# Block-causal attention followed by a channel mix: from two stages with x in DRAM to one interleaved program with x on chip

## The chip, the core and the metric

The kernel runs on one core of a Trainium2 chip. The core has five engines that run at the same time and wait for each other by semaphores: TensorE (PE, matrix multiplication; loads of its stationary operand are shown as PEld), VectorE (DVE), ScalarE (ACT), GpSimd (POOL) and SyncE (SP), which here only issues DMAs. Work passes through SBUF (128 partitions) and PSUM (8 banks of 128 x 2 KB), where matmul results land. The metric is device time of one execution in microseconds.

## The reference

There are 8 batches of 8 heads, 576 positions and 64 channels a head, all float32. Attention is causal by blocks of 64 positions. Its output, with the heads side by side as 512 channels, is x of a channel mix that shifts by one position:

```
S  = q k^T / 8, kept where i // 64 >= j // 64      # i the query, j the key
x  = (exp(S) / row sum) v                          # (8, 576, 512)
xk = mu_k x + (1 - mu_k) x_prev                    # x_prev: x one position earlier, 0 at the start of a batch
xr = mu_r x + (1 - mu_r) x_prev
out = sigmoid(xr w_r) * (relu(xk w_k)^2 w_v)       # w_k 512x1024, w_v 1024x512, w_r 512x512
```

Matmul operands are 16-bit, sums are float32.

## The kernel before

The program has two stages, one after the other.

**Stage 1, attention (lines 74 to 180), a loop over 8 batches.** q and k are loaded by GpSimd's queue with a cast to bfloat16 (lines 88 and 92), 128 positions to a partition tile, so that a row of 64 numbers is the unit that lies together. PE transposes them in blocks of 128 columns (line 103), VectorE copies the halves to KT and QT (lines 108, 110), both on partitions 0 to 63. v is loaded and cast the same way (lines 115, 119) beside columns of ones (line 122). Then a loop over 8 heads: six score matmuls (line 134) of keys against queries, 1600 columns in all, into one PSUM buffer; exp on ScalarE in two pieces (lines 147, 149); GpSimd zeroes what the mask removes (line 152); then PE multiplies with v as the stationary operand and exp as the moving one (lines 157, 162, 166), into one PSUM buffer PA. Row 64 of PA holds the row sums. ScalarE copies the 64 channel rows to XTB (line 169), VectorE the row sums to LTB (line 171). At a batch's end x, not yet normalised and transposed (channels on partitions), goes to DRAM with the row sums (lines 172, 173). After the last batch all row sums come back, VectorE takes reciprocals (line 179) and these go to DRAM.

**Stage 2, channel mix (lines 185 to 275), a loop over 4 pairs of batches.** SP loads x and, repeated over partitions, the reciprocals (lines 203, 207). VectorE multiplies them (line 216), GpSimd subtracts neighbours (DT, line 224), VectorE makes XK and XR (lines 226, 229). PE multiplies XK with WK (PK, line 238), ScalarE takes the relu (line 244), VectorE the square (line 246). Then for chunks of 128 positions: PR (line 261), sigmoid (line 265), PV (line 269), the product (line 273) and the store (line 275).

**What sets the order.** The program is written as loops over tiles from pools. The tile layer inserts the semaphores, and a planner orders each engine's instructions: program order is the priority, and an instruction whose inputs or buffers are late by the planner's own reckoning can be placed behind later ones. On the chip each engine, and each DMA queue, then runs its list in that fixed order. The order around the change is therefore the planner's, not one written by hand. A pool's `bufs` says how many tiles of a tag can be alive at once.

Of the kernel before, what the change touches and what calls it, by code (L numbers as in the profile page):

```python
# [9 lines left out]
FP = mybir.dt.float32  # L10
F16 = mybir.dt.float16
# [6 lines left out]
def kernel(  # L18
# [12 lines left out]
    nc = tc.nc  # L31
# [4 lines left out]
    SC = (H * S) // P  # L36
    CCn = C // P
    JCn = DF // P
    assert S == 576 and D == 64 and C == 512

    consts = ctx.enter_context(tc.tile_pool(name="consts", bufs=1))
    drams = ctx.enter_context(tc.tile_pool(name="drams", bufs=1, space=bass.MemoryType.DRAM))

    ident = consts.tile([P, P], BF)
    make_identity(nc, ident)

    xT_dram = drams.tile([P, CCn, B * S], FP)

    with tc.tile_pool(name="wstg", bufs=1) as wstg:
        WKs = wstg.tile([P, CCn, DF], FP)  # L50
        nc.sync.dma_start(WKs, moe_w_k.rearrange("(cc p) j -> p cc j", p=P))
        WK = consts.tile([P, CCn, DF], F16)
        nc.vector.tensor_copy(WK, WKs)
        WVs = wstg.tile([P, JCn, C], FP)
        nc.sync.dma_start(WVs, moe_w_v.rearrange("(cc p) j -> p cc j", p=P))
        WV = consts.tile([P, JCn, C], F16)
        nc.vector.tensor_copy(WV, WVs)
        WRs = wstg.tile([P, CCn, C], FP)
        nc.sync.dma_start(WRs, moe_w_r.rearrange("(cc p) j -> p cc j", p=P))
        WR = consts.tile([P, CCn, C], F16)  # L60
        nc.vector.tensor_copy(WR, WRs)
    MUK = consts.tile([P, CCn], FP)
    nc.sync.dma_start(MUK, moe_mu_k.rearrange("(cc p) -> p cc", p=P))
    MUR = consts.tile([P, CCn], FP)
    nc.sync.dma_start(MUR, moe_mu_r.rearrange("(cc p) -> p cc", p=P))
    l_dram = drams.tile([B * H, S], FP)
    ri_dram = drams.tile([B * H, S], FP)

    QS = [0, 128, 256, 384, 512]
    CS = [0, 576, 1024, 1344, 1536]  # L70
    NE = 1600
    ISQ = float(1.0 / (D ** 0.5))

    with (
        tc.tile_pool(name="qk", bufs=2) as qk_pool,
        tc.tile_pool(name="tr", bufs=2) as tr_pool,
        tc.tile_pool(name="vp", bufs=2) as v_pool,
        tc.tile_pool(name="ep", bufs=2) as e_pool,
        tc.tile_pool(name="xo", bufs=3) as xo_pool,
        tc.tile_pool(name="xtb", bufs=2) as xtb_pool,  # L80
        tc.tile_pool(name="pstr", bufs=2, space=bass.MemoryType.PSUM) as ps_tr,
        tc.tile_pool(name="pss", bufs=1, space=bass.MemoryType.PSUM) as ps_s,
        tc.tile_pool(name="psav", bufs=1, space=bass.MemoryType.PSUM) as ps_av,
    ):
        RB = 6
# [220 lines left out]
```

## Time and profile before

| | us |
|---|---|
| three runs | 501.98, 505.07, 505.12 |
| median | 505.07 |
| span of the profiled execution, first to last instruction | 498.2 |
| busy PE / VectorE / ScalarE / GpSimd in it | 368.1 / 268.6 / 212.6 / 156.1 |

Of the profiled execution the span is given and not its own device time. The three runs lie 3.8 to 6.9 us above that span.

How to read the profile: the page gives, for one execution, each engine's busy time, the span in 40 slices with the granted TensorE clock (PEclk, as a share of 2.4 GHz), the DMA queues and the groups of instructions that cost most. A group is named by line, engine, operation, and output <- inputs, with partitions x elements, its count, busy time and the mean duration of one. Matmuls are pipelined, and a matmul's duration has the drain of its result in it: 8 matmuls in a row take less than 8 durations. PE's busy time is the union of these durations, so a busy PE can still stream at half its rate. "Idle before" is the time in which an engine waited ahead of a group, with what ended the wait.

### The profile page before, as it was taken

The numbers are of one execution on the slowest core, as the hardware profiler recorded it, in microseconds if no ns is written. First come the engines' busy times: TensorE is split into PE (matmuls) and PEld (weight loads), VectorE is DVE, ScalarE is ACT, GpSimd is POOL, SyncE is SP. The second block draws the span as 40 slices with busy tenths as digits, with TensorE's granted clock in tenths as the row PEclk, the third lists the DMA queues.
The fourth block names the chain that finished last, engine by engine and source line by source line (L and its number), as shares of the span: only waits on it lengthen the run. The fifth ranks groups of instructions, "written<-read, shape, count | busy, mean of one in ns | idle before, by whom it ended". The sixth has DMA issues, their size and how long they took to land.

```text
span 498.2 us, 5776 instructions
## 1 busy us (share of the span) xinstructions
PE 368.1 (74%) x2112; PEld 194.4 (39%) x2112; DVE 268.6 (54%) x360; ACT 212.6 (43%) x330; POOL 156.1 (31%) x342
## 2 busy tenths in 40 slices
PE   0008798897979798889960005987968988999996
PEld 0005455463635455544430001543434434544642
DVE  2207544362726355632223159989799889625622
ACT  1002665665666658776640000731344125415621
POOL 9432417264454625341110035043343321000000
PEclk9999856675685759765555556998999999999999
DMA  9999999999499999191107989036882220121022
GB/s 284 215 133 108 126 32 147 94 140 100 104 122 86 131 36 145 23 123 39 59 18 278 269 215 289 0 91 179 234 225 45 95 78 7 42 107 42 22 93 75
DMA packets 132891, 57.95 MB, mean 116 GB/s; under 512 B 113784, under 2 KB 113784, under 8 KB 132856
## 3 DMA queue, kind: packets, MB, share of 16 engines
q0 software_dynamic: 111488, 14.16, 61.6%
q1 hardware_dynamic: 21376, 43.44, 29.1%
q8 instruction: 16, 0.26, 0.2%
q14 instruction: 11, 0.09, 0.1%
HBM read 52.58 MB, written 19.17 MB: 144 GB/s over the span
## 4 chain that ended last, share of the span: by engine, by line
PE 47%; DVE 19%; DMA 12%; ACT 9%; issue 7%; POOL 6%; SPq 0%; ACTq 0%; DVEq 0%; POOLq 0%
PE PV L269 11%; PE PA L157 9%; PE PS L134 9%; PE PK L238 6%; PE PR L261 5%; DVE K L246 4%; ACT E L147 4%; DVE XR L229 4%; DMA VO<-in_v_dram 4%; DVE LTB L171 4%; DVE XK L226 3%; PE pst L103 3%; ACT XTB L169 3%; DMA QKN<-in_k_dram 3%; DMA RB<-ri_dram 3%
## 5 line engine op out<-in xcount | busy, mean ns | idle before, releaser
L171 DVE COPY LTB<-PA 1x576 f32<-1x576 f32 x64 | 48.1, 751 | 109.3 <-ACT XTB L169 109.3
L238 PE MATMUL PK<-XK,WK 128*128 128x384 f16 (+2 forms) x384 | 67.5, 333 | 47.5 <-DVE XK L226 40.2
L147 ACT ACTIVATE E<-PS 128x1024 f16<-128x1024 f32 x64 | 65.5, 1023 | 82.4 <-PE PS L134 79.3
L134 PE MATMUL PS<-QT,KT 64*128 64x64 bf16 (+4 forms) x384 | 81.2, 362 | 9.5 <-ACT E L149 8.5
L269 PE MATMUL PV<-WV,K 128*128 128x512 f16 x320 | 76.7, 383 | 9.0 <-DVE OV L273 9.0
L157 PE MATMUL PA<-E,VO 128*128 128x512 f16 (+3 forms) x256 | 71.1, 421 | 14.7 <-DVE LTB L171 12.2
L244 ACT ACTIVATE KRj<-PK 128x512 f32<-128x512 f32 (+2 forms) x96 | 46.4, 491 | 81.1 <-PE PK L238 63.3
L224 POOL TENSOR_TENSOR DT<-XT 128x1154 f32<-128x1154 f32 x16 | 44.3, 2784 | 112.5 <-DVE XT L216 82.6
L238 PEld LDWEIGHTS <-WK 128*128 128x128 f16 x384 | 37.6, 98 | 77.3 <-issue 53.1
L152 POOL MEMSET E<- 64x64 f16 x256 | 29.3, 152 | 114.6 <-ACT E L147 99.8
L103 PE MATMUL pst<-ident,QKN 128*128 128x128 bf16 x288 | 31.1, 270 | 41.6 <-DMA QKN<-in_k_dram 38.6
L265 ACT ACTIVATE Rt<-PR 128x512 f32<-128x512 f32 (+1 forms) x40 | 23.7, 596 | 80.9 <-PE PR L261 55.3
L169 ACT COPY XTB<-PA 64x576 f32<-64x576 f32 x64 | 40.4, 631 | 35.3 <-PE PA L166 34.1
L134 PEld LDWEIGHTS <-KT 64*128 64x128 bf16 x384 | 38.1, 117 | 44.4 <-issue 30.6
L246 DVE TENSOR_TENSOR K<-KRj 128x512 f16<-128x512 f32 (+2 forms) x96 | 49.4, 567 | 3.1 <-ACT KRj L244 2.3
L269 PEld LDWEIGHTS <-K 128*128 128x128 f16 x320 | 31.5, 98 | 48.4 <-issue 12.1
L273 DVE TENSOR_TENSOR OV<-Rt,PV 128x512 f32<-128x512 f32 (+1 forms) x40 | 27.2, 683 | 38.4 <-PE PV L269 37.8
L157 PEld LDWEIGHTS <-VO 128*128 128x128 f16 x256 | 27.3, 125 | 49.8 <-issue 24.1
L261 PE MATMUL PR<-WR,XR 128*128 128x512 f16 x160 | 43.1, 390 | 3.8 <-DVE XR L229 3.8
L108 DVE COPY KT<-pst 64x768 bf16<-64x768 bf16 x48 | 26.4, 549 | 28.9 <-PE pst L103 28.0
L149 ACT ACTIVATE E<-PS 128x576 f16<-128x576 f32 x64 | 41.3, 645 | 0.0
L103 PEld LDWEIGHTS <-QKN 128*128 128x128 bf16 x288 | 22.7, 121 | 47.3 <-issue 44.0
(29 smaller groups left out, 289.7 us busy)
## 6 DMA issues: line engine op xcount, KB each, us to landing
xT_dram<-XTB SPq DMA_DIRECT2D x8, 1152.0 KB, 6.8
XTu<-xT_dram SPq DMA_DIRECT2D x8, 1152.0 KB, 8.0
RB<-ri_dram SPq DMA_DIRECT2D x16, 576.0 KB, 6.7
out_dram<-OV SPq DMA_DIRECT2D x32, 256.0 KB, 2.0
QKN<-in_q_dram POOLq DMA_DIRECT2D x8, 576.0 KB, 8.1
QKN<-in_k_dram POOLq DMA_DIRECT2D x8, 576.0 KB, 9.8
VO<-in_v_dram POOLq DMA_DIRECT2D x32, 128.0 KB, 8.9
WKs<-in_moe_w_k_dram SPq DMA_DIRECT2D x1, 2048.0 KB
```

Source lines behind the costliest of these rows:

```text
L103: nc.tensor.matmul(pst[:, i, :], QKN[:, blk + i, :, :].rearrange("p a b -> p (a b)"), ident, is_transpose=True, start=(i == 0), stop=(i == ...
L134: nc.tensor.matmul(PS[:, col:col + (q1 - q0)], KT[0:D, s0 + kc * P: s0 + (kc + 1) * P], QT[0:D, s0 + q0: s0 + q1], start=start, stop=stop)
L147: nc.scalar.activation(E[:, 0:1024], PS[:, 0:1024], AF.Exp, scale=ISQ)
L157: nc.tensor.matmul(PA[:, QS[kc]:512], Vc[:, kc], E[:, CS[kc]:CS[kc] + 512 - QS[kc]], start=(kc == 0), stop=(kc == 3))
L169: nc.scalar.copy(XTB[(h % 2) * D:(h % 2) * D + D, h // 2, :], PA[0:D, :])
L171: nc.vector.tensor_copy(LTB[0:1, h, :], PA[D:D + 1, :])
L224: nc.gpsimd.tensor_tensor(DT[:, 1:TT], XT[:, cc, 1:TT], XT[:, cc, 0:TT - 1], ALU.subtract)
L238: nc.tensor.matmul(PK[:, 0:t1 - t0], WK[:, cc, jc * P:(jc + 1) * P], XK[:, cc, t0:t1], start=(cc == 0), stop=(cc == CCn - 1))
L244: nc.scalar.activation(KRj[:, 0:t1 - t0], PK[:, 0:t1 - t0], AF.Relu)
L246: nc.vector.tensor_tensor(K2[:, jc, t0:t1], KRj[:, 0:t1 - t0], KRj[:, 0:t1 - t0], ALU.mult)
L261: nc.tensor.matmul(PR, XR[:, cc, ws:ws + P], WR[:, cc, :], start=(cc == 0), stop=(cc == CCn - 1))
L269: nc.tensor.matmul(PV, K2[:, jc, ws:ws + P], WV[:, jc, :], start=(jc == 0), stop=(jc == JCn - 1))
```

## The change

The two stages become one program of slots, 13 to a batch.

- q and k are loaded through SP's queue in float32, six positions of a head to a partition, so that 1536 bytes lie together; v as well, in rows of 256 bytes. GpSimd casts them to 16 bit. Two heads share the 128 partitions of QT and KT: even heads on 0 to 63, odd heads on 64 to 127.
- Scores of a pair of heads are made in three pieces of 2 x 512 columns; the last block of 64 keys of all heads of a batch is one more piece. exp takes 1024 columns at a time.
- For the product with v, exp tiles of 128 keys x 128 queries are the stationary operand and v with a column of ones (65 columns) the moving one. So queries are on partitions, the row sum is a column, and VectorE normalises out of PSUM. The last key block's exp lies in a tile that is zero elsewhere.
- x stays in SBUF. PE transposes it (float32) into chunks of 512 positions that run on across batches; each chunk keeps the column ahead of it.
- The weights are cast by the DMA; sigmoid(z) becomes (tanh(z / 2) + 1) / 2, with the half folded into WV.
- A batch's attention pieces are written alternately with the channel-mix matmuls ("units") of the chunk before, at slots given by hand; the planner still orders each engine from that. All PSUM but the scores' comes from one pool of four one-bank buffers (tag m).

The core of the diff (removed lines are those printed above):

```diff
+    ld_pool = pool("ld", 4)
+    vl_pool = pool("vl", 3)
...
+    kr_pool = pool("kr", 3)
+    k2_pool = pool("k2", 1)
+    o_pool = pool("op", 3)
+    ps_s = pool("pss", 2, space=PSUM)
+    ps_m = pool("psm", 4, space=PSUM)
...
+    VOs = [consts.tile([P, 5, H, D1 + 1], F16, name=f"VO{i}") for i in range(2)]
+    E4s = [consts.tile([P, H, P], F16, name=f"EL{i}") for i in range(2)]
+    QN, KN, QT, KT = {}, {}, {}, {}
...
+    def load_qk(b):
+        for hh in range(2):
+            for n, src in enumerate((q, k)):
+                LD[b, n, hh] = ld_pool.tile([PQ, HP, R, D], FP, tag="ld",
+                                            name="LD")
+                for h in range(0, HP, 2):
+                    nc.sync.dma_start(
+                        LD[b, n, hh][:, h:h + 2],
+                        src[b, hh * HP + h:hh * HP + h + 2].rearrange(
+                            "h (p r) d -> p h r d", r=R))
+    def cast_qk(b, hh, h):
+        for n, (dst, tag) in enumerate(((QN, "qn"), (KN, "kn"))):
+            if h == 0:
+                dst[b, hh] = qk_pool.tile([PQ, R, HP, D], BF, tag=tag, bufs=2,
+                                          name="QKN")
+            nc.gpsimd.tensor_copy(
+                dst[b, hh][:, :, h:h + 2].rearrange("p r h d -> p h r d"),
+                LD[b, n, hh][:, h:h + 2])
...
+    def load_v(b):
+        for sc in range(5):
+            n = P if sc < 4 else D
+            VL[b, sc] = vl_pool.tile([P, H, D], FP, tag="vl", name="VL")
+            nc.sync.dma_start(
+                VL[b, sc][0:n],
+                v[b, :, sc * P:sc * P + n].rearrange("h p d -> p h d"))
+    def cast_v(b, sc):
+        n = P if sc < 4 else D
+        nc.gpsimd.tensor_copy(VOs[b % 2][0:n, sc, :, 0:D], VL[b, sc][0:n])
...
+    def load_w():
+        nc.gpsimd.dma_start(WK, moe_w_k.rearrange("(cc p) j -> p cc j", p=P))
+        nc.gpsimd.dma_start(WR, moe_w_r.rearrange("(cc p) j -> p cc j", p=P))
+        nc.gpsimd.dma_start(WV, moe_w_v.rearrange("(cc p) j -> p cc j", p=P))
+        nc.vector.tensor_scalar_mul(WV, WV, 0.5)
+        nc.vector.tensor_scalar_add(MUK, MUK, -1.0)
+        nc.vector.tensor_scalar_add(MUR, MUR, -1.0)
+    def qk_transpose(b, pr):
+        if pr == 0:
+            QT[b] = tr_pool.tile([P, HP, S], BF, tag="qt", name="QT")
+            KT[b] = tr_pool.tile([P, HP * S + D], BF, tag="kt", name="KT")
+            nc.vector.memset(KT[b][:, HP * S:], 0.0)
+        for which in range(2):
+            N = (QN, KN)[which][b, pr // 2]
+            pst = ps_m.tile([P, CH], FP, tag="m", name="PQK")[:, :].bitcast(BF)
+            view = pst[:, 0:S].rearrange("p (r t) -> p t r", r=R)
+            for r in range(R):
+                nc.tensor.matmul(
+                    pst[:, r * PQ:(r + 1) * PQ], N[:, r, pr % 2 * 2:pr % 2 * 2 + 2, :].rearrange(
+                        "p h d -> p (h d)"),
+                    identb[0:PQ, 0:PQ], is_transpose=True,
+                    start=(r == 0), stop=(r == R - 1))
+            if which == 0:
+                nc.scalar.copy(
+                    QT[b][:, pr].rearrange("p (t r) -> p t r", r=R), view)
+            else:
+                    KT[b][:, pr * S:(pr + 1) * S].rearrange(
+                        "p (t r) -> p t r", r=R), view)
+    PIECES = [
+        [(0, 0, 0, 512)],
+        [(0, 0, 512, 64), (64, 1, 128, 448)],
+        [(0, 2, 256, 320), (320, 3, 384, 192)],
+    ]
+    ZEROS = [[0], [64], [0, 320]]
+    EP = {}
+    def score(b, pr, i):
+        if i == 0:
+            EP[b, pr] = e_pool.tile([P, 2, 3, 512], F16, tag="e", name="E")
+        E = EP[b, pr]
+        PS = ps_s.tile([P, 2, 512], FP, tag="s", name="PS")
+        for (col, kc, q0, n) in PIECES[i]:
+            for h in range(2):
+                rows = slice(h * D, h * D + D)
+                nc.tensor.matmul(
+                    PS[:, h, col:col + n],
+                    KT[b][rows, pr * S + kc * P: pr * S + (kc + 1) * P],
+                    QT[b][rows, pr, q0:q0 + n], start=True, stop=True)
+        nc.scalar.activation(E[:, :, i, :], PS, AF.Exp, scale=ISQ)
+        for z in ZEROS[i]:
+            nc.gpsimd.memset(E[D:P, :, i, z:z + D], 0.0)
+    def score_last(b):
+        E4 = E4s[b % 2]
+        PS = ps_s.tile([P, 2, 512], FP, tag="s", name="PS4")
+        for pr in range(HP):
+            for h in range(2):
+                rows = slice(h * D, h * D + D)
+                nc.tensor.matmul(
+                    PS[:, h, pr * D:pr * D + D],
+                    KT[b][rows, pr * S + 512: pr * S + 640],
+                    QT[b][rows, pr, 512:576], start=True, stop=True)
+        nc.scalar.activation(
+            E4[0:D, :, D:P].rearrange("p (a h) q -> p h a q", h=2),
+            PS[0:D, :, 0:HP * D].rearrange("p h (a q) -> p h a q", q=D),
+            AF.Exp, scale=ISQ)
+    def stationary(b, h, kc, m):
+        E = EP[b, h // 2][:, h % 2].rearrange("p i n -> p (i n)")
+        if kc == 4:
+            return E4s[b % 2][:, h, :]
+        base = (0, 576, 1024, 1344)[kc]
+        c = base + (448 if m == 4 else m * P) - kc * P
+        return E[:, c:c + P]
+    def av_norm(b, h):
+        if h == 0:
+            x_all[b] = x_pool.tile([P, 5, C], FP, tag="x", name="X")
+        VO = VOs[b % 2]
+        PA = ps_m.tile([P, CH], FP, tag="m", name="PA")
+        for m in range(5):
+            for kc in range(m + 1):
+                nc.tensor.matmul(
+                    PA[:, m * D1:(m + 1) * D1], stationary(b, h, kc, m),
+                    VO[:, kc, h, 0:D1], start=(kc == 0), stop=(kc == m))
+        Rc = r_pool.tile([P, 5], FP, tag="r", name="Rc")
+        view = PA[:, 0:5 * D1].rearrange("p (m e) -> p m e", e=D1)
+        nc.vector.reciprocal(Rc, view[:, :, D])
+        nc.vector.tensor_tensor(
+            x_all[b][:, :, h * D:(h + 1) * D], view[:, :, 0:D],
+            Rc[:, :].unsqueeze(2).to_broadcast([P, 5, D]), ALU.mult)
+    def x_transpose(b, m):
+        g0 = b * S + m * P
+        rows = P if m < 4 else D
+        off = 0 if m < 4 else D
+        px = ps_m.tile([P, CH], FP, tag="m", name="PX")
+        for cc in range(CCn):
+            nc.tensor.matmul(
+                px[:, cc * P:(cc + 1) * P],
+                x_all[b][:, m, cc * P:(cc + 1) * P], identf,
+                is_transpose=True, start=(cc == 0), stop=(cc == CCn - 1))
...
+            nc.scalar.copy(XT[c][:, :, 1 + t:1 + t + n],
+                           view[:, :, off + done:off + done + n])
+            done += n
+    def mix(c):
+        x = XT[c]
+        XK = xk_pool.tile([P, CCn, CH], F16, tag="xk", name="XK")
+        XR = xk_pool.tile([P, CCn, CH], F16, tag="xr", name="XR")
+        for cc in range(CCn):
+            DT = d_pool.tile([P, CH], FP, tag="d", name="DT")
+            nc.gpsimd.tensor_tensor(DT, x[:, cc, 1:CH + 1], x[:, cc, 0:CH],
+                                    ALU.subtract)
+            for b in range(B):
+                t = b * S - c * CH
+                if 0 <= t < CH:
+                    nc.gpsimd.tensor_copy(DT[:, t:t + 1],
+                                          x[:, cc, t + 1:t + 2])
+            for (dst, mu) in ((XK, MUK), (XR, MUR)):
+                    dst[:, cc], DT, mu[:, cc:cc + 1],
+                    x[:, cc, 1:CH + 1], ALU.mult, ALU.add)
+        XKR[c] = (XK, XR)
+    def pk(c, jc):
+        if jc == 0:
+            K2[c] = k2_pool.tile([P, JCn, CH], F16, tag="k2", name="K2")
+        ps = ps_m.tile([P, CH], FP, tag="m", name="PK")
+        for cc in range(CCn):
+            nc.tensor.matmul(ps, WK[:, cc, jc * P:(jc + 1) * P],
+                             XKR[c][0][:, cc], start=(cc == 0),
+                             stop=(cc == CCn - 1))
+        KR = kr_pool.tile([P, CH], FP, tag="kr", name="KR")
+        nc.scalar.activation(KR, ps, AF.Relu)
+        nc.vector.tensor_tensor(K2[c][:, jc], KR, KR, ALU.mult)
+    def prr(c, jt):
+        ps = ps_m.tile([P, CH], FP, tag="m", name="PR")
+        for cc in range(CCn):
+            nc.tensor.matmul(ps, XKR[c][1][:, cc, jt * P:(jt + 1) * P],
+                             WR[:, cc], start=(cc == 0), stop=(cc == CCn - 1))
+        T[c, jt] = t_pool.tile([P, CH], FP, tag="t", name="T")
+        nc.scalar.activation(T[c, jt], ps, AF.Tanh, scale=0.5)
+    def pv(c, jt):
+        ps = ps_m.tile([P, CH], FP, tag="m", name="PV")
+        for jc in range(JCn):
+            nc.tensor.matmul(ps, K2[c][:, jc, jt * P:(jt + 1) * P],
+                             WV[:, jc], start=(jc == 0), stop=(jc == JCn - 1))
+        OV = o_pool.tile([P, CH], FP, tag="o", name="OV")
+        nc.vector.scalar_tensor_tensor(OV, T[c, jt], 1.0, ps, ALU.add,
+                                       ALU.mult)
+        g = c * CH + jt * P
+        nc.sync.dma_start(o2[g:g + P], OV)
+    NP_ = 13
+    slots = {}
+    def at(slot, fn, *args):
+        slots.setdefault(slot, []).append((fn, args))
+    for b in range(B):
+        s0 = b * NP_
+        order = [("s", 0, 0), ("s", 0, 1), ("s", 0, 2), ("l",)] + [
+            ("s", pr, i) for pr in range(1, HP) for i in range(3)]
+        for n, o in enumerate(order):
+            if o[0] == "l":
+                at(s0 + n, score_last, b)
+            else:
+                at(s0 + n, score, b, o[1], o[2])
+            if b + 1 < B:
+                if n == 0:
+                    at(s0, load_qk, b + 1)
+                if n in (3, 5, 7, 9):
+                    at(s0 + n, cast_qk, b + 1, (n - 3) // 4, (n - 3) % 4)
+                if n == 3 and b == 0:
+                    at(s0 + n, load_w)
+                if n == 4:
+                    at(s0 + n, load_v, b + 1)
+                if n in (8, 9, 10, 11, 12):
+                    at(s0 + n, cast_v, b + 1, n - 8)
+                if n in (6, 8, 10, 12):
+                    at(s0 + n, qk_transpose, b + 1, (n - 6) // 2)
+        for pr in range(HP):
+            done = 3 if pr == 0 else 3 + 3 * pr
+            at(s0 + done + 2, av_norm, b, 2 * pr)
+            at(s0 + done + 3, av_norm, b, 2 * pr + 1)
+        for m in range(5):
+            at(s0 + NP_ + 3 + (m + 1) // 2, x_transpose, b, m)
+        at(s0 + NP_ + 5, mix, b)
+    at(B * NP_ + 5, mix, NCH - 1)
+    units = []
+    for c in range(NCH):
+        first = (c + 1) * NP_ + 7 if c < NCH - 1 else B * NP_ + 7
+        us = [(pk, c, jc) for jc in range(JCn)]
+        us += [(prr, c, 0), (prr, c, 1), (pv, c, 0), (prr, c, 2), (pv, c, 1),
+               (prr, c, 3), (pv, c, 2), (pv, c, 3)]
+        for i, u in enumerate(us):
+            units.append((first + i * NP_ / len(us), u))
+    qk_transpose(0, 0)
+    for pr in range(1, HP):
+        at(pr - 1, qk_transpose, 0, pr)
+    nu = 0
+    for s in range(max(slots) + 1):
+        todo = slots.get(s, [])
+        mine = []
+        while nu < len(units) and units[nu][0] < s + 1:
+            mine.append(units[nu][1])
+            nu += 1
+        for i in range(max(len(todo), len(mine))):
+            if i < len(todo):
+                fn, args = todo[i]
+                fn(*args)
+            if i < len(mine):
+                mine[i][0](*mine[i][1:])
+    for _, u in units[nu:]:
+        u[0](*u[1:])
```

## Rows read from the trace of the kernel before

**Rows 1.** The page's parts 1 and 2: busy us (share) xinstructions; the clock in 40 slices.

```profile
PE 368.1 (74%) x2112; PEld 194.4 (39%) x2112; DVE 268.6 (54%) x360; ACT 212.6 (43%) x330; POOL 156.1 (31%) x342
...
PEclk9999856675685759765555556998999999999999
```

**Rows 2.** Windows by stage: window, length, busy us of each engine (x instructions), granted clock, DMA share, GB/s.

```profile
37.00:258.00 221.00, 192.14 (x1241) 108.84 (x1242) 100.29 (x168) 139.44 (x191) 89.18 (x304) 0.67 1.21 91
258.00:298.00 40.00, 1.20 (x9) 0.84 (x8) 12.79 (x5) 0.63 (x1) 4.18 (x2) 0.50 0.83 238
298.00:494.00 196.00, 174.54 (x864) 84.69 (x863) 148.63 (x182) 71.20 (x137) 40.16 (x14) 0.96 0.35 103
```

**Rows 3.** Waits: who waited <- for whom: us in total, times, longest us.

```profile
PE PK L238 <- DVE XK L226: 40.2, 4, 38.9
PE pst L103 <- DMA QKN<-in_k_dram: 38.6, 2, 37.0
...
DVE WK L53 <- DMA WKs<-in_moe_w_k_dram: 8.7, 1, 8.7
```

**Rows 4.** Chain of waits, channel mix at its end: start us, us, what.

```profile
471.76 1.73 PE PV L269 x8
```

**Rows 5.** Timeline of PE and its loads, 39 to 52 us: start us, us, engine, line, what xcount.

```profile
39.78 0.60 PE L134 MATMUL PS<-QT,KT 64*128 64x512 bf16 x1
...
49.27 0.84 PE L134 MATMUL PS<-QT,KT 64*128 64x512 bf16 x6
...
50.04 0.67 PEld L103 LDWEIGHTS <-QKN 128*128 128x128 bf16 x12
...
51.44 0.21 PEld L162 LDWEIGHTS <-VO 128*128 128x128 f16 x4
```

**Rows 6.** Groups of ScalarE by form, with busy us, mean ns | idle; then its timeline.

```profile
L147 ACT ACTIVATE E<-PS 128x1024 f16<-128x1024 f32 x64 | 65.5, 1023 | 82.4 <-PE PS L134 79.3 <-POOL E L152 1.9
...
L169 ACT COPY XTB<-PA 64x576 f32<-64x576 f32 x64 | 40.4, 631 | 35.3 <-PE PA L166 34.1
...
L244 ACT ACTIVATE KRj<-PK 128x512 f32<-128x512 f32 x32 | 18.9, 597 | 66.9 <-PE PK L238 61.9 <-DVE K L246 5.0
...
325.35 1.28 ACT L265 ACT_TABLE_LOAD   x1
```

**Rows 7.** Groups of VectorE by form.

```profile
L108 DVE COPY KT<-pst 64x768 bf16<-64x768 bf16 x48 | 26.4, 549 | 28.9 <-PE pst L103 28.0
...
L273 DVE TENSOR_TENSOR OV<-Rt,PV 128x512 f32<-128x512 f32 x32 | 21.7, 683 | 28.9 <-PE PV L269 28.4 <-issue 0.2 <-DMA out_dram<-OV 0.2
```

**Rows 8.** Timeline of VectorE and GpSimd, 290 to 312 and 404 to 416 us.

```profile
292.69 4.18 POOL L224 TENSOR_TENSOR DT<-XT 128x1154 f32<-128x1154 f32 x2 [36.24 <-DVE XT L216]
294.83 3.25 DVE L226 SCALAR_TENSOR_TENSOR XK<-DT,MUK,XT 128x1154 f16<-128x1154 f32 x1 [2.37 <-POOL DT L224]
...
298.00 1.41 DVE L229 SCALAR_TENSOR_TENSOR XR<-DT,MUR,XT 128x1154 f16<-128x1154 f32 x1
...
311.07 1.29 DVE L246 TENSOR_TENSOR K<-KRj 128x512 f16<-128x512 f32 x2
...
408.87 0.69 DVE L273 TENSOR_TENSOR OV<-Rt,PV 64x512 f32<-64x512 f32 x1
...
407.65 5.66 POOL L224 TENSOR_TENSOR DT<-XT 128x1154 f32<-128x1154 f32 x2 [8.81 <-DVE XR L229]
```

**Rows 9.** Groups of GpSimd by form.

```profile
L152 POOL MEMSET E<- 64x64 f16 x256 | 29.3, 152 | 114.6 <-ACT E L147 99.8 <-ACT E L149 13.9
L122 POOL MEMSET VO<- 128x2560 f16 x8 | 17.9, 2243 | 0.3
```

**Rows 10.** The page's part 3, DMA queues: packets, MB, share of 16 engines.

```profile
q0 software_dynamic: 111488, 14.16, 61.6%
q1 hardware_dynamic: 21376, 43.44, 29.1%
```

**Rows 11.** A window of 4 us late in attention, columns as in rows 2.

```profile
224.00:228.00 4.00, 3.88 (x18) 1.81 (x18) 0.89 (x2) 2.83 (x4) 0.69 (x6) 0.50 0.01 4
```

More of the change, by code (lines that the diff above doesn't have):

```diff
@@ L35 @@
     P = 128
-    SC = (H * S) // P
+    HP = H // 2
     CCn = C // P
     JCn = DF // P
-    assert S == 576 and D == 64 and C == 512
[L41 to L61, printed above, removed]
+    R = 6
@@ new lines, in cast_v @@
+    def cast_v(b, sc):
+        n = P if sc < 4 else D
+        nc.gpsimd.tensor_copy(VOs[b % 2][0:n, sc, :, 0:D], VL[b, sc][0:n])
+    load_qk(0)
+    for pr in range(HP):
+        cast_qk(0, pr // 2, pr % 2 * 2)
+    for i in range(2):
+        nc.vector.memset(VOs[i][:, :, :, D:D1], 1.0)
+        nc.vector.memset(VOs[i][D:P, 4], 0.0)
+        nc.vector.memset(E4s[i], 0.0)
+    load_v(0)
+    for sc in range(5):
+        cast_v(0, sc)
+    WK = consts.tile([P, CCn, DF], F16)
+    WR = consts.tile([P, CCn, C], F16)
@@ new lines @@
+    XT = {}
+    def x_transpose(b, m):
[8 more added lines that the diff above has]
+                is_transpose=True, start=(cc == 0), stop=(cc == CCn - 1))
+        view = px[:, :].rearrange("p (c t) -> p c t", t=P)
+        done = 0
+        while done < rows:
+            c, t = divmod(g0 + done, CH)
+            n = min(rows - done, CH - t)
+            if c not in XT:
+                XT[c] = xt_pool.tile([P, CCn, CH + 1], FP, tag="xt", name="XT")
+                if c == 0:
+                    nc.vector.memset(XT[c][:, :, 0:1], 0.0)
+                else:
+                    nc.vector.tensor_copy(XT[c][:, :, 0:1],
+                                          XT[c - 1][:, :, CH:CH + 1])
+            nc.scalar.copy(XT[c][:, :, 1 + t:1 + t + n],
+                           view[:, :, off + done:off + done + n])
+            done += n
@@ new lines, in prr @@
+    def prr(c, jt):
[5 more added lines that the diff above has]
+        nc.scalar.activation(T[c, jt], ps, AF.Tanh, scale=0.5)
+    o2 = out.rearrange("b s c -> (b s) c")
+    def pv(c, jt):
[8 more added lines that the diff above has]
+        nc.sync.dma_start(o2[g:g + P], OV)
@@ new lines @@
+    NP_ = 13
[9 more added lines that the diff above has]
+                at(s0 + n, score_last, b)
+            else:
+                at(s0 + n, score, b, o[1], o[2])
[12 more added lines that the diff above has]
+                    at(s0 + n, qk_transpose, b + 1, (n - 6) // 2)
+        for pr in range(HP):
+            done = 3 if pr == 0 else 3 + 3 * pr
[4 more added lines that the diff above has]
+        at(s0 + NP_ + 5, mix, b)
```

222 lines of the change are left out of this document (29 added, 193 removed).

## The prediction

> **What bounds the kernel now.** I read the page first, then busy time by stage, the waits, and the timeline. The page shows a TensorE (PE) that counts as busy for 74% of the span, at a granted clock that swings between half and full until the second stage [rows 1]. Windows cut by what PE does split the span into 37 us until the first q/k tile has come, 221 us of attention, 40 us in which PE does almost nothing, and 196 us of channel mix [rows 2]. The waits name both gaps: PE's transposes wait 37.0 us at once for a k load, and the first channel-mix matmul 38.9 us for XK, while x and the row sums go to DRAM and come back [rows 3]. In attention PE is busy 87% of the time at a mean clock of 0.67; in channel mix 89%, at 0.96 [rows 2]. So the old time is two serial stages, two gaps of some 76 us together, and a first stage at two thirds of the clock.
>
> **PE's work in the new kernel, at full clock.** Prices come from stretches in which PE ran without a stop. Channel mix: 8 matmuls of 512 columns take 1.73 us [rows 4], 0.216 us each. Nine chunks of 512 tokens need 32 PK, 16 PR and 32 PV matmuls each: 720, so 155.5 us.
> Scores: still 1600 columns a head. By the price of a column above that is 0.676 us (six took 0.84 us with the last one's drain [rows 5]); 64 heads, 43.3 us.
> Attention times V: 15 matmuls a head, each of 65 columns behind a load of 128 fresh columns of exp. Twelve loads of 128 columns with their matmuls took 0.67 us, four loads ahead of 64-column matmuls 0.21 us [rows 5]: 0.054 us a pair, set by the load. 960 of them are 52 us; the old form streamed the same 1600 columns a head as the scores, 43 us. This part of the change alone costs 9 us.
> q/k transposes: 384 at 0.056, 21.5 us. x transposes: 160 in float32, which no row shows. Not under the bf16 price (0.056) and, as four passes, not over 0.224: 9 to 36 us; I take twice the bf16 price for twice the bytes, 18 us.
> Sum: 290 us (281 to 308).
> The Trainium skill, "TensorE: Matmul & The Clock Gate", section Back-to-back issue gap, gives about 81 ns per pair of load and 128-column matmul in a real kernel. That would put 35 us on the 1,344 pairs and make my total some 394 us; the row (56 ns) disagrees and is used.
>
> **What lies beside PE.** ScalarE: 96 exps of 1024 columns at 1.023, 72 relus, 36 tanhs and 8 small exps at 0.597, 32 QT copies at 0.631, about 45 x copies at up to 0.597 [rows 6]: 98 + 69 + 20 + 26 = 213 us. That is 26.7 us per batch under PE's 34 to 36, so it costs nothing while PE runs; without that cover it would be the next bound. If tanh needed another table than exp, 36 changes there and back would cost 72 loads of 1.28 us, the price at the old kernel's first sigmoid [rows 6]: 92 us on ScalarE, which brings it level with PE. I take 0, and the high end of the range holds it.
> The Trainium skill, "ScalarE: Activation LUTs", section Table sets, puts tanh into exp's set; no row here shows a tanh. By it the 92 us are 0 too.
> VectorE: 32 KT copies of 576 columns out of PSUM (0.549 for 768 without a stride, 0.683 for 512 in float32 [rows 7], take 0.65), 64 reciprocals with a 320-column multiply out of PSUM (0.65 together, worked down from the same 0.683), 72 mixes and 72 squares of 512 at 0.645 (two squares took 1.29 [rows 8]), 36 outputs at 0.683: 21 + 42 + 46 + 46 + 25 = 180 us, 22 per batch.
> GpSimd loses the issue of 56 loads and gains casts: 64 of 768 elements and 40 of 512, 69,632 elements. Not under a memset's 0.876 ns an element (2.243 us for 2560), not over the 1.84 of the two-input subtract (2.12 us for 1154): 61 to 128 us. A cast has one input, so I take 1.1 ns, 77 us. Subtracts: 36 x 512 x 1.84 = 34 us. Zeroing: 128 memsets at about 0.2 us, 26 us [rows 8, 9]. Sum 137 us (121 to 188), 17 per batch.
> Here is a collision: with a subtract running on GpSimd, VectorE's mix took 3.25 us, and 1.41 with the next beside no subtract; the GpSimd op stretched too [rows 8]. They take turns. VectorE's output multiply, one operand in PSUM, kept 0.69 us beside a subtract [rows 8]. So mixes and squares (11.5 us a batch) queue with all of GpSimd's work: 28.5 us a batch, at most 35. That is under PE's, with little room.
> DMA: x's trip out and back goes. The v rows stay 256 bytes: 8 x 576 x 8 = 36,864 packets. At the 44 ns that the present small packets cost (61.6% of 16 engines' span over 111,488 [rows 10]) that is 13 us a batch. q, k and outputs are 16,896 rows of 1.5 and 2 KB; at the 108 ns of the other queue's packets [rows 10] they take 14. Together 27, under 34, so hidden.
> New waits: all loads but the weights', and all stores, sit on SP's queue. v's fourth and fifth loads wait for a staging buffer, and output stores queue behind them; three output buffers cover that, and VectorE would wait if they ran out. A GpSimd cast that waits for its load holds back the memset that AV of that head needs; two slots of the 13 to a batch (5 us) cover it. VectorE's scaling of WV waits for a 5 MB load at the start, with PSUM evacuations behind it unless the planner puts it later: 0 to 20 us, I take 0 within the start below.
>
> **The sum.** Start: 1.2 MB of q and k (the old kernel's first 2 MB were there at 8.7 us [rows 3]) and two casts, then transposes: first score at 10 us, where it was 39.8 [rows 5]. Slots 0 to 19 hold attention alone: PE work of 25 us at full clock, 50 at half; ScalarE needs 25. Attention alone ran at 0.67 [rows 2], so I take 40 us. From there channel mix fills PE's waits. Left are 290 - 25 = 265 us of PE work; nothing in the trace shows such a mixture, so I take the 89%, rounded to 0.9, at which the channel-mix stage keeps PE busy beside a loaded VectorE [rows 2]: 295 us. Last output and its store: 3 us. Span 348 us. The profiled execution's own time is given only as its span, 498.2; the median of the runs, 505.07, lies 6.9 us above (3.8 to 6.9 for the three runs). So **355 us**.
>
> **Rivals.**
> A. Scores in halves overlap. Consecutive score matmuls now use rows 0 to 63 and 64 to 127 and two PSUM banks. In the old kernel all used rows 0 to 63, so the trace shows neither; the floor is half, 21.7 us for 43.3. Divided by 0.9 that is 24 us off: 331, and 306 with float32 transposes at the low price and a start at full clock.
> The Trainium skill, "TensorE: Matmul & The Clock Gate", Part 3, says that matmuls on different row groups run concurrently. By that A is the case; no row here bears on it.
> B. VectorE and GpSimd become the bound. For it: the 3.25 us row. Against it: the 0.69 us row. At the upper GpSimd price the pair has 35 us a batch; at 90% that is 39, times 8, with 50 + 3 + 7: 372. If every VectorE op took turns (22 + 23.5 a batch) it would be 424.
> C. Slower: the clock. For it: late in attention PE was busy for 3.88 of 4 us and stayed at the lower level, 0.50 [rows 11]. Half of the new PE work is of that kind, and AV streams only 65 columns per load. At half clock throughout, 290 us become 580, in all about 600. The point where it decides: 20 us around it and 290/c, so 505 is passed at a mean clock below 0.60. Against it: at half clock PE would be the only bound, with channel-mix matmuls always ready, and the channel-mix stage ran at 0.96 even at 89% busy [rows 2].
> D. The change does not do what it says: the planner moves instructions whose inputs are late, so pieces might not alternate. Attention alone at 0.67 clock would take some 200 us and channel mix 173 after it: about 390, still faster.
>
> **How the numbers follow.** Forecast, PE bound at mostly full clock: 0.50. A 0.27, B 0.12, D 0.04, C 0.07 (0.05 of it beyond 505). Bounds of the forecast's own terms: 9 us down and 20 up for x transposes, 15 down and 10 (20 with the WV wait) up for the start, and PE at 95% or 80%, 16 down and 36 up. The range takes in most of A and of B: 310 to 420. One per cent is 5 us, about what a measurement of this kernel can tell from no change: faster 0.94, same 0.01, slower 0.05.
>
> **What would show it.** Right: the gaps of 37 and 38.9 us gone; the granted clock near 1.0 from about 50 us on; PE the largest share of the chain; AV loads at 0.05 to 0.06 us each. Score pairs that start within some ns of each other speak for A. PE waits released by VectorE, and mixes of 1.5 us and more, speak for B. Matmuls of 512 columns at 0.43 us in the middle of the kernel speak for C. The prediction is wrong if casts take over 1.5 us each, if ScalarE loads tables again and again, or if PE waits on DMA.

## The result, and the profile after

The changed kernel takes 351.88 us (median of 4 runs, 350.84 to 353.24) against 504.32 us: a ratio of 0.700, interval 0.696 to 0.704. The forecast was 355 us. The profiled execution took 352.34 us with a span of 350.6, so 1.7 us lie around the span, not 6.9. Ratios leave out three executions over 1.5% longer than the fastest of their kernel (928.37 us of the run with all units in one slot, 355.85 of the run with later units, 511.12 of the old kernel without staging tiles), which the medians below still hold.

The page of the kernel after, parts 1 and 2:

```profile
PE 289.2 (83%) x2608; PEld 155.6 (44%) x2608; DVE 212.8 (61%) x366; ACT 197.0 (56%) x289; POOL 161.4 (46%) x311
...
PE   2750784889939996999699959997999999849995
...
PEclk9999995899958998999879998999899999998999
```

Two windows, the start and the middle (columns as in rows 2):

```profile
0.00:60.00 60.00, 30.90 (x365) 19.53 (x366) 23.07 (x46) 29.76 (x38) 34.80 (x73) 0.94 0.97 215
...
60.00:290.00 230.00, 207.93 (x1989) 112.11 (x1987) 153.71 (x269) 147.49 (x217) 114.81 (x225) 0.93 0.39 107
```

Beside [rows 1, 2]: PE's busy time fell from 368 to 289 us, the clock is near 1.0 with dips that come back about every 36 us (the digits 5 to 8 in the PE and PEclk lines), and the first 60 us keep PE busy for half of the time only. In the first 39 us or so PE is slower than that clock says; the products of a head with v in the chain of waits (start us, us, what) show it:

```profile
36.30 0.84 PE PA L225 x15
...
42.31 0.46 PE PA L225 x15
...
59.35 0.83 PE PA L225 x15
```

At 59 us the recorded clock is 0.50, at 42 it is 1.0, and at 36 the same 15 products take as long as at 59 although the record reads 1.0. The gaps of 37 and 38.9 us [rows 3] are gone. PE's waits in the kernel after are these (columns as in rows 3):

```profile
PE PK L292 <- DVE OV L315: 16.7, 4, 5.8
PE PQK L155 <- POOL QKN L98: 16.7, 7, 5.0
PE PA L225 <- POOL VO L114: 8.1, 3, 4.8
PE PA L225 <- DVE X L231: 5.2, 2, 3.0
```

The largest are released by VectorE's output multiply OV (4 times, up to 5.8 us) and by GpSimd's casts. The waits for casts all lie in the first 60 us, where the loads they need are late; after that PE waits for VectorE, 27.7 us in all.

PE at full clock, in a stretch without a wait (timeline, columns as in rows 5):

```profile
118.90 0.39 PE L185 MATMUL PS<-QT,KT 64*128 64x64 bf16 x4
119.23 0.60 PE L225 MATMUL PA<-VO,E 128*128 128x65 f16 x14
119.67 0.19 PE L225 MATMUL PA<-VO,EL 128*128 128x65 f16 x1
119.70 1.89 PE L312 MATMUL PV<-WV,K 128*128 128x512 f16 x8
121.52 0.39 PE L185 MATMUL PS<-QT,KT 64*128 64x320 bf16 x4
121.84 1.04 PE L302 MATMUL PR<-WR,XR 128*128 128x512 f16 x4
122.72 0.60 PE L243 MATMUL PX<-identf,X 128*128 128x128 f32 x4
123.15 1.03 PE L312 MATMUL PV<-WV,K 128*128 128x512 f16 x4
```

The durations of neighbours overlap, so a price is read from start to start: a score piece of 1024 columns 0.33 us, 15 products of a head with v 0.47 us, 8 PV matmuls 1.82, a PR group 0.88, four float32 transposes 0.43.

And a chunk's start, where PE stops (timeline of three engines):

```profile
92.64 0.67 DVE L315 SCALAR_TENSOR_TENSOR OV<-T,PV 128x512 f32<-128x512 f32 x1
...
93.24 0.74 DVE L280 SCALAR_TENSOR_TENSOR XR<-DT,MUR,XT 128x512 f16<-128x512 f32 x1
...
94.12 1.42 POOL L272 TENSOR_TENSOR DT<-XT 128x512 f32<-128x512 f32 x1 [1.69 <-DVE XR L280]
...
94.56 1.52 DVE L280 SCALAR_TENSOR_TENSOR XR<-DT,MUR,XT 128x512 f16<-128x512 f32 x1
...
96.72 0.75 DVE L280 SCALAR_TENSOR_TENSOR XK<-DT,MUK,XT 128x512 f16<-128x512 f32 x1 [0.64 <-POOL DT L277]
...
97.17 1.20 POOL L272 TENSOR_TENSOR DT<-XT 128x512 f32<-128x512 f32 x1
97.39 1.53 DVE L280 SCALAR_TENSOR_TENSOR XR<-DT,MUR,XT 128x512 f16<-128x512 f32 x1
...
99.55 0.75 DVE L280 SCALAR_TENSOR_TENSOR XK<-DT,MUK,XT 128x512 f16<-128x512 f32 x1 [0.63 <-POOL DT L277]
...
100.22 0.75 DVE L280 SCALAR_TENSOR_TENSOR XR<-DT,MUR,XT 128x512 f16<-128x512 f32 x1
...
100.99 0.65 DVE L315 SCALAR_TENSOR_TENSOR OV<-T,PV 128x512 f32<-128x512 f32 x1
...
101.69 4.85 PE L292 MATMUL PK<-XK,WK 128*128 128x512 f16 x11 [5.84 <-DVE OV L315]
```

From 93.2 to 100.9 us VectorE does nothing but mixes, seven of a chunk's eight. Two XR that start while a subtract runs take 1.52 us where the others take 0.75, and two XK wait 0.6 us for GpSimd. The evacuation of the last PV, OV, stands behind them until 100.99. Then PE starts again, after 5.84 us, at some 0.43 us a matmul, twice the price at full clock [rows 4]; the granted clock from 101.7 to 107 us is 0.50.

The groups that answer to the forecast's prices (columns as in rows 7):

```profile
L98 POOL CAST QKN<-LD 96x768 bf16<-96x768 f32 x64 | 58.5, 944 | 23.3 <-PE PQK L155 7.4 <-issue 7.4 <-DMA LD<-in_k_dram 5.0
...
L272 POOL TENSOR_TENSOR DT<-XT 128x512 f32<-128x512 f32 x36 | 42.4, 1186 | 25.4 <-DVE XR L280 14.1 <-issue 6.0 <-ACT XT L259 4.0
...
L280 DVE SCALAR_TENSOR_TENSOR XR<-DT,MUR,XT 128x512 f16<-128x512 f32 x36 | 38.4, 1067 | 0.0
...
L280 DVE SCALAR_TENSOR_TENSOR XK<-DT,MUK,XT 128x512 f16<-128x512 f32 x36 | 30.6, 851 | 18.2 <-POOL DT L277 17.7
...
L161 ACT ACT_TABLE_LOAD x1 | 1.3, 1283 | 0.7 <-PEq L399 0.7
```

### The profile page after: what moved, and what is told of

The parts are those of the page before. It is cut to its first block, busy times and chain, and to the rows that moved or that the text cites. A ratio compares the mean times of both kernels' runs of the same rounds, so it can differ in the third digit from the quotient of the medians.

```text
span 350.6 us, 6713 instructions
## 1 busy us (share of the span) xinstructions
PE 289.2 (83%) x2608; PEld 155.6 (44%) x2608; DVE 212.8 (61%) x366; ACT 197.0 (56%) x289; POOL 161.4 (46%) x311
## 4 chain that ended last, share of the span: by engine, by line
PE 56%; DVE 14%; POOL 11%; DMA 7%; issue 4%; ACT 4%; SPq 2%; POOLq 0%; DVEq 0%; ACTq 0%
PE PK L292 20%; PE PV L312 10%; PE PR L302 8%; PE PA L225 7%; POOL DT L272 6%; DMA LD<-in_k_dram 6%; DVE XR L280 5%; PE PS L185 5%; DVE XK L280 4%; PE PQK L155 3%; SPq L88 2%; DVE OV L315 2%; POOL QKN L98 2%; ACT E L189 2%; PE PX L243 2%
## 5 line engine op out<-in xcount | busy, mean ns | idle before, releaser
L189 ACT ACTIVATE E<-PS 128x1024 f16<-128x1024 f32 x96 | 97.0, 1028 | 41.0 <-PE PS L185 25.1
L292 PE MATMUL PK<-XK,WK 128*128 128x512 f16 x288 | 81.5, 427 | 18.7 <-DVE OV L315 16.7
L297 DVE TENSOR_TENSOR K<-KR 128x512 f16<-128x512 f32 x72 | 56.8, 801 | 25.7 <-ACT KR L296 25.0
L296 ACT ACTIVATE KR<-PK 128x512 f32<-128x512 f32 x72 | 43.0, 600 | 52.2 <-PE PK L292 43.9
L98 POOL CAST QKN<-LD 96x768 bf16<-96x768 f32 x64 | 58.5, 944 | 23.3 <-PE PQK L155 7.4
L272 POOL TENSOR_TENSOR DT<-XT 128x512 f32<-128x512 f32 x36 | 42.4, 1186 | 25.4 <-DVE XR L280 14.1
L225 PE MATMUL PA<-VO,E 128*128 128x65 f16 x896 | 39.6, 197 | 10.5 <-DVE X L231 5.2
L225 PEld LDWEIGHTS <-E 128*128 128x128 f16 x896 | 35.0, 100 | 22.0 <-issue 8.3
L185 PE MATMUL PS<-QT,KT 64*128 64x512 bf16 (+4 forms) x320 | 41.9, 322 | 3.3 <-ACT E L189 3.1
L155 PE MATMUL PQK<-identb,QKN 96*128 96x96 bf16 x384 | 27.2, 223 | 18.8 <-POOL QKN L98 16.7
L280 DVE SCALAR_TENSOR_TENSOR XK<-DT,MUK,XT 128x512 f16<-128x512 f32 x36 | 30.6, 851 | 18.2 <-POOL DT L277 17.7
L280 DVE SCALAR_TENSOR_TENSOR XR<-DT,MUR,XT 128x512 f16<-128x512 f32 x36 | 38.4, 1067 | 0.0
L305 ACT ACTIVATE T<-PR 128x512 f32<-128x512 f32 x36 | 21.5, 596 | 21.0 <-PE PR L302 21.0
```

The lines of the kernel that those rows point to most:

```text
L98: nc.gpsimd.tensor_copy(dst[b, hh][:, :, h:h + 2].rearrange("p r h d -> p h r d"), LD[b, n, hh][:, h:h + 2])
L155: nc.tensor.matmul(pst[:, r * PQ:(r + 1) * PQ], N[:, r, pr % 2 * 2:pr % 2 * 2 + 2, :].rearrange("p h d -> p (h d)"), identb[0:PQ, 0:PQ], i ...
L185: nc.tensor.matmul(PS[:, h, col:col + n], KT[b][rows, pr * S + kc * P: pr * S + (kc + 1) * P], QT[b][rows, pr, q0:q0 + n], start=True, sto ...
L189: nc.scalar.activation(E[:, :, i, :], PS, AF.Exp, scale=ISQ)
L225: nc.tensor.matmul(PA[:, m * D1:(m + 1) * D1], stationary(b, h, kc, m), VO[:, kc, h, 0:D1], start=(kc == 0), stop=(kc == m))
L272: nc.gpsimd.tensor_tensor(DT, x[:, cc, 1:CH + 1], x[:, cc, 0:CH], ALU.subtract)
```

## Experiments

Times of different runs are compared through their ratios to the kernel before, measured beside each; 0.01 is 5 us.

**Do the score matmuls of a pair overlap?** (rival A)

```diff
-rows = slice(h * D, h * D + D)
+rows = slice(0, D)          # in score and score_last
```

> Left out: odd heads read the q and k rows of their even neighbours, so that both heads of a pair score on rows 0 to 63; all else is as in the changed kernel. Rival A (the two score matmuls of a pair overlap): the pair of pieces that took 0.32 to 0.33 us takes 0.43 us or more; over 96 pieces and 32 small pairs that is 10 to 20 us of PE work, and the time rises by 5 to 20 us. The price in the forecast's sum (no overlap): nothing changes, within 3 us.

362.77 us, ratio 0.723 (0.719 to 0.726): 11 to 12 us more than the changed kernel's 0.700. PE is busy for 310.2 us, 21.0 more. A piece now takes 0.54 us from start to start where it took 0.33:

```profile
125.21 0.61 PE L185 MATMUL PS<-QT,KT 64*128 64x320 bf16 x4
125.75 1.04 PE L302 MATMUL PR<-WR,XR 128*128 128x512 f16 x4
```

Rival A's mechanism holds: on different rows the two halves run at the same time. Of 21 us of PE work about half shows in the time; the rest falls into waits that were there anyway.

**What does a pair of load and 65-column matmul cost?**

```diff
-        for m in range(5):
+        for m in list(range(5)) * 2:      # in av_norm
```

> Each head's 15 products of exp and v are made twice over, the second time over the first: 960 more pairs of load and 65-column matmul and no work for another engine. If a pair costs the 0.054 us of the forecast and PE is the bound: 52 us more work, divided by 0.9 some +55 us. If a pair costs the 0.031 us that 15 of them took in the changed kernel's trace (0.47 us): 30 us of work, +25 to +33 us. If VectorE's queue sets the end and PE has room: under +15 us.

366.96 us, ratio 0.732 (0.727 to 0.736): 16 us more, between the last two expectations, and PE's busy time 24.3 us more, 25 ns a pair. The price of 0.054 us is refuted, 0.03 confirmed, and a third of the added work disappears in PE's waits.

**Is PE late at a chunk's start because XK is late, or because VectorE's queue is held?**

```diff
-        first = (c + 1) * NP_ + 7 if c < NCH - 1 else B * NP_ + 7
+        first = (c + 1) * NP_ + 10 if c < NCH - 1 else B * NP_ + 10
```

> Channel-mix units start three slots later (10 for 7), nothing else. Theory L (PE waits at a chunk's start because XK is not made yet): the waits of 3 to 6 us at each of seven chunk starts go, -15 to -30 us. Theory V (the mix's 8 operations hold VectorE's queue for some 12 us, the PSUM evacuations behind them come late, the four PSUM buffers fill and PE stops whatever it is to do next): the waits move to other matmuls, 0 to -8 us.

354.93 us, ratio 0.704 (0.699 to 0.710): no gain. PE's waits moved from PK to other matmuls, as theory V has it (columns as in rows 3; PK for OV is 4.8 us in all here, where it was 16.7):

```profile
PE PR L302 <- DVE OV L315: 9.5, 3, 5.3
...
PE PA L225 <- DVE OV L315: 4.2, 1, 4.2
```

Theory L falls.

```diff
-        at(s0 + NP_ + 5, mix, b)
+        for cc in range(CCn):            # mix takes one cc at a time
+            at(s0 + NP_ + 5 + cc, mix, b, cc)
...  (units as in the run before; the last chunk's mix in slots 9 to 12)
```

> The mix of a chunk is written in four parts, one per slot (slots 5 to 8), and units start three slots later as in the run before. Theory V: evacuations get between the parts, PE's waits released by VectorE fall from some 25 us to under 10, and the time falls by 15 to 30 us. Theory L: no more than the run with later units alone gains.

343.04 us, ratio 0.683 (0.680 to 0.686): 8 us less. V is supported, but gives half of what it promised at the least: PE's waits released by VectorE fell from 28 to 21 us, not to under 10.

**Do VectorE and GpSimd take turns at a price?**

```diff
-            nc.gpsimd.tensor_tensor(DT, x[:, cc, 1:CH + 1], x[:, cc, 0:CH],
+            nc.vector.tensor_tensor(DT, x[:, cc, 1:CH + 1], x[:, cc, 0:CH],
...  (the one-column copies to DT move too)
```

> The subtract of neighbours (DT) and its one-column copies move from GpSimd to VectorE, nothing else. Theory V with turns (a mix waits for its own subtract and for whatever GpSimd runs meanwhile): VectorE gets 25 us more work, but a mix falls from 0.85 and 1.07 us on average to some 0.75, and the chain of a chunk's mix from about 12 us to 8 or 9; -3 to -12 us. Rival (VectorE's plain load sets the end, turns do not matter): +5 to +25 us.

334.26 us, ratio 0.667 (0.664 to 0.670): 17 us less, although VectorE has more to do:

```profile
L280 DVE SCALAR_TENSOR_TENSOR XR<-DT,MUR,XT 128x512 f16<-128x512 f32 x36 | 29.0, 804 | 0.0
...
L272 DVE TENSOR_TENSOR DT<-XT 128x512 f32<-128x512 f32 x36 | 24.2, 712 | 0.0
```

The second mix of a pair fell from 1.07 to 0.80 us and the subtract from 1.19 on GpSimd to 0.71 on VectorE. It gained more than expected, and not by a shorter chain: a chunk's mix lasted 7.2 to 9.4 us from its first operation on VectorE to its last (chunks 2 to 8), and lasts 9.2 to 10.4 here, with the subtracts in it. What changed is the order: more evacuations now stand among the mixes, in the second chunk these two, where the changed kernel has the one at 92.64 us:

```profile
93.74 0.68 DVE L315 SCALAR_TENSOR_TENSOR OV<-T,PV 128x512 f32<-128x512 f32 x1
...
101.11 0.48 DVE L231 TENSOR_TENSOR X<-PA,Rc 128x320 f32<-128x320 f32 x1
```

PE's waits released by VectorE fell from 28 to 17 us, those released by GpSimd from 25 to 20, and the first PK came at 56.4 us for 60.0. The edit does three things at once: no mix meets a subtract, VectorE no longer waits for GpSimd ahead of XK (18.2 us before), and GpSimd's casts have 42 us of subtracts less ahead of them. This run does not separate them, so it doesn't price the turns.

That the two engines take turns is shown by single instructions in the traces. In the changed kernel 32 mixes met neither a subtract nor a cast and took 0.745 us on average; 15 XR that started into a running subtract took 1.45. Of 18 XK that were already running when a subtract started 15 kept 0.74 to 0.75, so it is the later one that waits: the subtracts took 1.04 us or, 15 of them, 1.20 to 1.42. In the run with the subtract moved, 63 mixes that met no cast took 0.746 and the nine that met one 1.18, which accounts for the mean of 0.80.

Both edits together (the two diffs above, each mix with its subtract on VectorE):

> Both edits at once: the subtract on VectorE, and the mix in four parts with units three slots later. If both remove the same wait (VectorE's queue held at a chunk's start): no further than the better of the two, 331 to 337 us. If the turns with GpSimd and the unbroken run of mixes are separate costs: they add up, 324 to 329 us.

321.0 us, ratio 0.639 (0.636 to 0.643): 30 us under the changed kernel, where the two alone gave 8 and 17, and below both expectations. Their gains add up, and some 5 us more come from their acting together. Windows of the middle, first of the run with the subtract moved, then of both:

```profile
60.00:290.00 230.00, 217.07 (x2084) 119.59 (x2084) 175.41 (x349) 152.70 (x229) 76.60 (x172) 0.97 0.40 111
```

```profile
60.00:290.00 230.00, 222.85 (x2108) 118.98 (x2106) 184.82 (x364) 153.91 (x232) 78.92 (x172) 0.98 0.41 113
```

PE is busy for 208, 217 and 223 of the same 230 us, at 0.93, 0.97 and 0.98 of the clock: the dips at chunk starts go with the waits.

**The start.**

```diff
-                if n == 3 and b == 0:
+                if n == 9 and b == 0:
                     at(s0 + n, load_w)
```

> The weights' loads are written at slot 9 of batch 0 in place of slot 3. In the changed kernel PE is nearly idle from 21 to 35 us while k of batch 1 waits behind 5 MB of weights. Theory S (order of the loads makes that stall): k of batch 1 lands near 20 us and the time falls by 8 to 14 us. Rival (the first 12 MB have to come before channel mix starts in any order): the stall moves to the first PK, 0 to -3 us.

355.64 us, ratio 0.709 (0.706 to 0.712): 5 us more, which neither theory had. The edit moved less than it says: GpSimd issued WK and WR at 13.4 and 17.4 us, where it had been 12.8 and 16.1, for the planner kept them early; only WV went from 17.7 to 29.1. So neither theory was tried in full. The chain of waits of this run shows where the 5 us come from (start us, us, what):

```profile
29.09 12.83 DMA WV<-in_moe_w_v_dram
41.94 1.23 DVE WV L140
43.16 0.41 DVE X L231
```

VectorE waited for WV until 41.94 us and scaled it until 43.16, with an evacuation behind it, and PE waited 7.5 us for that. So I took the scaling away, on top of the moved subtract:

```diff
-        nc.vector.tensor_scalar_mul(WV, WV, 0.5)
...
-        nc.scalar.activation(KR, ps, AF.Relu)
+        nc.scalar.activation(KR, ps, AF.Relu, scale=0.5 ** 0.5)
```

> The subtract on VectorE, the weights' loads at slot 9, and no scaling of WV on VectorE: the half goes into relu's scale (root of a half). With late weights alone VectorE stood at the scaling of WV until 41.9 us, and PE waited 7.5 us for an evacuation behind it. If that wait is what ate the gain of late weights: 8 to 14 us under the run with the subtract moved, 320 to 326 us. If the start is bound by the bytes that have to come before channel mix in any order: 332 to 337 us.

328.59 us, ratio 0.656 (0.652 to 0.659): 5.6 us under 0.667, between the two expectations. Here too only WV was late (issued at 28.0 us, WK and WR at 12.8 and 16.7). A late WV without the scaling gains, but less than the 14 us of the stall: PE still waits 5.9 us for v's cast before 27.4 us. The scaling taken away by itself was not tried, so what the later load adds is open.

All of these edits in one kernel (units later, mix one piece at a time, subtract and one-column copies on VectorE, load of the weights written later, scaling folded into the relu):

```diff
-                if n == 3 and b == 0:
+                if n == 9 and b == 0:
...
+                nc.vector.tensor_tensor(DT, x[:, cc, 1:CH + 1], x[:, cc, 0:CH],
...
+        for cc in range(CCn):
+            at(s0 + NP_ + 5 + cc, mix, b, cc)
```

> All the edits together (subtract on VectorE, mix in four parts and later units, weights late, no scaling of WV). The better of the last two runs, or up to 8 us under it if the edits act in different stretches: 316 to 332 us.

314.18 us, ratio 0.628 (0.624 to 0.632), 36 us under the changed kernel and the best of all. In the middle PE is busy for 98% of the time at full clock:

```profile
0.00:60.00 60.00, 36.80 (x419) 23.40 (x420) 25.13 (x57) 32.02 (x41) 34.27 (x73) 0.91 0.99 215
...
60.00:290.00 230.00, 224.40 (x2109) 120.03 (x2106) 183.83 (x364) 155.58 (x237) 78.15 (x170) 1.00 0.41 114
```

PE's waits released by VectorE follow the times, in the profiled executions: 28 us in the changed kernel, 26 with later units, 21 with the mix split, 17 with the subtract moved, 8 with both, 5 here.

**Does the alternation written by hand matter?** (rival D)

```diff
-            units.append((first + i * NP_ / len(us), u))
+            units.append((first, u))
```

> All 16 units of a chunk are written into one slot (the one at which they started), so the program no longer alternates them with attention pieces. If the alternation written by hand carries the gain: scores wait for exps without filler, the clock falls in attention, +25 to +60 us. If the planner's own order fills PE's waits anyway: within 8 us.

379.56 us, ratio 0.756 (0.752 to 0.760): 28 us more. From 60 to 300 us the clock is 0.90. The planner alone does not get there, but it keeps 124 of the 152 us of the gain. The size is in the expected range, the reason is mostly another: PE waits 5.1 us for exps (3.1 in the changed kernel), but 25.9 for XK, where it waited 0.6:

```profile
PE PK L292 <- DVE XK L280: 25.9, 21, 3.2
```

Units written into one slot come before the mix has made what they need.

**Is the old kernel's late start worth its length?** Its staging tiles go and GpSimd's queue casts the weights:

```diff
-        WKs = wstg.tile([P, CCn, DF], FP)
-        nc.sync.dma_start(WKs, moe_w_k.rearrange("(cc p) j -> p cc j", p=P))
-        nc.vector.tensor_copy(WK, WKs)
+    nc.gpsimd.dma_start(WK, moe_w_k.rearrange("(cc p) j -> p cc j", p=P))
...  (WV and WR alike)
```

> The kernel before, with its weights cast by three DMAs of GpSimd's queue, without float32 staging tiles and VectorE's casts. The q and k tiles then need not wait for the staging memory: their issue moves from 22.5 us to some 5 us and the first transpose from 37 us to 18 to 25 us. The time falls by 12 to 20 us if the start counts one to one; if attention catches up in any case, by under 5 us.

499.12 us, ratio 0.993 (0.990 to 0.996). One more run of it gives the trace:

> The kernel before without staging tiles once more, for a profile: 497 to 500 us. If its attention is held by something that does not depend on the start (loads of the next batch through GpSimd's queue, or a lower clock), the first transposes come some 15 us sooner, and the last product of attention less than 5 us sooner than the 258.6 us of before.

497.91 us. Its chain begins so:

```profile
6.01 21.30 DMA QKN<-in_k_dram
34.62 9.34 DMA QKN<-in_k_dram
54.45 9.21 DMA QKN<-in_k_dram
76.98 8.97 DMA QKN<-in_k_dram
```

The first transpose comes at 27.4 us, 9.6 sooner and not the 12 to 19 that were expected, and attention's last product starts at 253.9 where it started at 259.0, 5.0 sooner: the next batches' k loads now stand in the chain, with 9 us each. So the old start was worth 3 to 4 us of its length; the loads behind it would have held attention for most of the rest. That the loads in long rows through SP let the early start count was not tried by itself.

## Why the prediction was right, and where it was not

- **The time** was 3 us off, inside the range. That is largely luck. PE's work was put 39 us too high, 33 of them after the start, which are 37 us of the forecast's time, and the time around the span 5 us too high; the share of PE's time took back 29, the start 10. Of the forecast's own signs the gaps and the clock came true. The loads of the products with v at 0.05 to 0.06 us did not, PE did wait on DMA in the first 60 us, and the signs of both A (score pairs start 3 to 4 ns apart) and B (waits released by VectorE, mixes of 1.5 us) came.
- **PE's work** was put too high. From starts in the trace: channel mix 155.5 us as forecast [rows 4]; scores 96 x 0.32 and 8 small pieces, 33 for 43.3; products with v 64 x 0.44 (0.42 to 0.47), 28 for 52; q/k transposes 12 in 0.5 to 0.6 us, some 18 for 21.5; x transposes 160 x 0.107, 17 for 18. Together 251 for 290 us. Gaps between groups, up to 0.14 us behind the products of a head, are not in it.
- **The step that failed worst** is "0.054 us a pair, set by the load". I read 0.21 us for four loads [rows 5] as a rate. It is the union of overlapping durations, with one load's latency of about 0.1 us in it; next to 64-column matmuls only the starts say what a pair costs. The old trace held them: the four matmuls behind those loads start 29 ns apart (51.492, 51.521, 51.550, 51.579 us). Doubling the pairs gave 25 ns each. So the new form of the product is cheaper than the 43 us that the prediction put for the old one, not dearer. The 81 ns of the Trainium skill, "TensorE: Matmul & The Clock Gate", section Back-to-back issue gap, for a pair with a 128-column matmul are not borne out either: 56 ns [rows 5]. Pairs with 65 columns, for which that figure is not given, take 29 ns (0.44 us for 15).
- **Scores** were priced without overlap because no old row showed two row halves. The run with both heads on the same rows shows it: 0.54 us against 0.33. The Trainium skill, "TensorE: Matmul & The Clock Gate", Part 3, was right here, and 21 us of PE work hang on it, 11 to 12 us of the time.
- **The share of PE's time** was put too high as well. From 60 to 347 us there are 232 us of work, 81%, where I took 90%: 287 us in place of 258. Of the 55 us between, PE stood idle for 29, and the other 26 lie in its busy time, at the lower clock and in gaps between groups. The idle time is the mechanism of rival B, as a wait and not as a load: VectorE was busy for 61% of the span only, but in order, and at a chunk's start the mixes, seven in a row in the chunk shown, stood ahead of the evacuations, slowed by turns with GpSimd and by waits for it. The Trainium skill, "GPSIMD Engine Reference", section Specifications, has the two engines contend where a VectorE instruction has two SBUF inputs. The trace agrees (a mix that starts into a subtract 1.45 us on average for 0.745; OV, with one operand in PSUM, 0.68 beside a subtract and 0.68 without) and gives the price, which the page does not. That the queue holds PE is shown by moving the subtract (17 us), splitting the mix (8 us) and both (30 us); later units alone (0 us) show that XK's lateness is not the cause. How much of the 17 us the turns are is open. By the prices above PE's work is 185 of the 230 us from 60 to 290 us (80%), 206 (89%) with both edits and 212 (92%) with all: the 0.9 was there once the stops were gone.
- **Rival C** is there in small: PE falls to half clock at these stops, for some 34 of the 287 us (mean clock 0.94), far from the 0.60 at which it would decide. With the stops gone the middle ran at 1.00.
- **The start**: first score at 9.65 us, forecast 10. Channel mix began at 60.0 us, forecast 50: k of batch 1 arrives late, which the chain of waits shows as one step:

```profile
21.02 13.48 DMA LD<-in_k_dram
```

   "VectorE's scaling of WV ... with PSUM evacuations behind it" cost nothing visible in the changed kernel, where WV was there at 33.7 us and the loads of k were the later event, and 7.5 us in the run with a late WV.
- **Beside PE**: casts 0.94 us (forecast 0.84), subtracts 1.19 (0.94), mixes 0.85 and 1.07 (0.645), squares 0.80 (0.645), one table load in all. The planner did keep the pieces alternating (rival D falls), and the order by hand is worth 28 of the 152 us.

## What to carry to other kernels

Price a stream of small matmuls by starts, not by the busy time of a few. When an engine that evacuates PSUM also runs a long chain for the next stage, its share of busy time says little (61% here): look what stands in its queue ahead of the evacuations at the moment PE stops, and split that chain, or move the part that another engine blocks. Read in the trace where a moved instruction went: a planner can leave it where it was, as it did with two of three weight loads here. An earlier start only counts where the next loads are there as well.

## What I had not expected of the hardware

Loads of 128 columns ahead of 65-column matmuls sustain 25 to 29 ns a pair. A mix that starts into a GpSimd subtract takes 1.52 us for 0.75, and one beside a cast 1.18; a subtract moved onto the busier VectorE made the kernel 17 us faster, of which the turns are a part of unknown size. Float32 transposes of 128 columns take 0.107 us, twice the 0.056 of bf16 [rows 5].
